# Block attention with a gated feed-forward: probabilities multiplied by their inverse sums ahead of the transpositions, and one gelu handed out earlier

## The chip, the cores and the metric

The kernel runs on one core of a Trainium2 chip. The metric is the device time of the whole program in microseconds (us). A core has five engines with a queue of instructions each: TensorE (PE) for matrix products and transpositions, VectorE (DVE), ScalarE (ACT), GpSimd (POOL) and SyncE (SP), which here only issues the transfers between the chip's memory (HBM) and the core's SBUF. TensorE writes into PSUM, eight banks of 128 partitions by 512 numbers of fp32, and DVE and ACT bring its results from there into SBUF.

## What is computed

Block-causal attention over eight batches of eight heads, 576 positions of 64 numbers, and behind it a gated feed-forward network with a spatial product. Everything is fp32. The reference, cut to what matters (the loads and reshapes are left out):

```python
scores = q @ k.T / sqrt(64)                    # 576 x 576 of each head
scores = where(block_i >= block_j, scores, -1e9)   # blocks of 64 positions
attn = exp(scores - max(scores))
attn = attn / (sum(attn) + 1e-9)
x = attn @ v                                   # (8, 576, 512) over all heads
h = gelu_tanh(x @ w_in)                        # 512 -> 1024
u, v = h[..., :512], h[..., 512:]
v_n = (v - mean(v)) / sqrt(var(v) + 1e-6) * g_ln
v_s = w_sg @ v_n + b_sg                        # over the 576 positions
out = x + (u * v_s) @ w_out
```

The probabilities may be divided by their sums ahead of the product with v, or the product behind it: the result is the same but for rounding.

## The kernel before

**Slots.** The attention goes through 32 slots, n = 0 to 31. A slot is a pair of heads of one batch, so four slots (`Q`) make a batch. Slots 0 to 3 run `opening_slot`, all others `slot`. Products that need fp32 are made of three fp32r products, of a high and a low part of each operand (`kh`, `kl`, `qh`, `ql`, `xh`, `xl`, `gh`, `gl`, `vh`, `vl`), and the low part is a subtraction, mostly on POOL.

**Tiles of probabilities.** The scores of a head lie in five tiles of rows, `prob0` to `prob4`: 64 rows by 64 columns, and then 128 rows by 192, 320, 448 and 576 columns; `pairs[i]` holds both heads' tiles i beside each other. There is one buffer of each, so the scores of slot n + 1 go into the tiles of slot n as soon as those have been transposed. For each tile and head DVE finds the maximum while it moves the scores out of PSUM (`maximum`, which leaves the negative maximum in `negm`), and ACT makes the exponentials in place and their row sums beside them in `sums` (`exponent`).

**A slot, in TensorE's order.** `turn("A0")` and `turn("A1")` transpose the four full blocks of `prob4` of each head into a bank (`pA`), which ACT (A0) and DVE (A1) copy to SBUF (`ptA`). A first hole follows, then `B0` and `B1` (blocks of `prob3` and `prob1`, to `pB` and `ptB`), a second hole, `C` (`prob2`), and `turn_sums`. A third hole, and the scores of slot n + 1: tiles 4, 1 and 0 (`first`). Then the products of slot n with v (`products`, into `ob` and the 64 columns `o0`), `normalise`, and the scores of tiles 3 and 2 (`second`). `inverse` of slot n + 1 and `split_qk(n + 2)` on POOL follow, and a fourth hole. A hole is filled with groups of the feed-forward network of the batch before: 5 groups of v (`accv`), 8 of u (`accu`), 8 of the output of the batch before that (`acco`) and 8 of the spatial product (`accs`). `PLAN` says how many groups each hole of the four slots of a batch takes: "1112", "2114", "2114", "2114".

**The sums.** `inverse` adds 1e-9 to the ten columns of sums, takes the reciprocal (`r`), and ACT spreads each of the ten columns to 64 (`rx`, 128 x 640). `turn_sums` makes ten transpositions: five of the diagonal blocks of `prob` and two of `rx` into the bank `pd`, three of `rx` into the bank `pe`. ACT copies both to `rb` (512 and 384 columns). So `rb` has in each column of positions the inverse sum, along the partitions of the head it belongs to, and `normalise` multiplies `ob` and `o0` by it.

**The side queue.** `side` holds what DVE, ACT and POOL have to do for the feed-forward: an entry "G" for a gelu (of the five tiles `vv`, later of the four tiles `u`), and behind that of v the statistics of its five tiles (`moments`: a `bn_stats` and a `bn_aggr` each), `inverse_std`, the five centrings (`centre`) and the five scalings (`scale`, which makes `vh`, `vl`, `vone` and `vn_t`). `run_gelu` takes a "G" if one stands in front, `run_side(k)` takes up to k other entries and stops at a "G". In `slot`, `run_gelu` is called once, behind the third hole, and `run_side` behind the other three holes with k = 3 (6 in the second batch).

**What sets the order.** TensorE's instructions stay in program order throughout. Those of DVE, ACT and POOL do so in slots 0 to 3; later a scheduler orders them by a timeline of its own, but for the few that are pinned by hand. All calls through a helper (`pin`) carry line 60 in the profile, so tiles, not lines, tell them apart. The banks of PSUM are taken in turn by one name, so a transposition or product waits until the eviction of the tile eight banks earlier is done.

Of the kernel before, what the change touches and what calls it, by code (L numbers as in the profile page):

```python
# [9 lines left out]
F32 = mybir.dt.float32  # L10
# [3 lines left out]
AF = mybir.ActivationFunctionType  # L14
ALU = mybir.AluOpType
# [5 lines left out]
def kernel(  # L21
# [13 lines left out]
    B, H, D, S = qT.shape  # L35
    P = 128
    BLK = 64
# [4 lines left out]
    NT = (S + P - 1) // P  # L42
# [5 lines left out]
    QN = [BLK] + [P] * (NT - 1)  # L48
# [3 lines left out]
    class Engine:  # L52


        def __init__(self, letter, engine):
            self.letter, self.engine = letter, engine
# [5 lines left out]
    vector = Engine("V", nc.vector)  # L62
    scalar = Engine("A", nc.scalar)
    gpsimd = Engine("G", nc.gpsimd)
# [3 lines left out]
    sp = ctx.enter_context(tc.tile_pool(name="sp", bufs=1))  # L68
# [7 lines left out]
    def page(dtype, n, name):  # L76
        tag, bufs = KINDS.get(name, KINDS["w"])
        return sp.tile([P, n], dtype, tag=tag, name=name, bufs=bufs)

    def bank(name):  # L80
        return psum.tile([P, 512], F32, tag="bank", name=name, bufs=8)
# [7 lines left out]
    def turn(out, in_):  # L89
        return tensor.transpose(out, in_, ident)  # L90

    def copy(e, dst, src):
        f = {"v": vector.tensor_copy, "a": scalar.copy, "g": gpsimd.tensor_copy}[e]
        return f(dst, src)
# [9 lines left out]
    def load_qk(n):  # L104
        b, h = PAIRS[n]
        q_f = sp.tile([P, S], F32, tag="q_f", name="q_f", bufs=1)
        k_f = sp.tile([P, S], F32, tag="k_f", name="k_f", bufs=1)
        nc.sync.dma_start(q_f, qT[b, h : h + 2].rearrange("a d s -> (a d) s"))
        nc.sync.dma_start(k_f, kT[b, h : h + 2].rearrange("a d s -> (a d) s"))
        raw[n] = (q_f, k_f)  # L110
# [15 lines left out]
    def load_v(n):  # L126
        b, h = PAIRS[n]
        v_f, v_d = vals[n] = v_bufs[n % 2]
        lo, hi = slice(0, BLK), slice(BLK, P)
        for a, r in ((0, lo), (1, hi)):  # L130
            cols = slice((h + a) * D, (h + a + 1) * D)
            x = v[b, : (NT - 1) * P, cols].rearrange("(j p) d -> p j d", p=P)
            if a == 0:
                nc.sync.dma_start(v_f[:, :, r], x)
            else:
                nc.sync.dma_start(v_f[lo, :, r], x[hi])
                nc.sync.dma_start(v_f[hi, :, r], x[lo])
            nc.sync.dma_start(v_d[r, : NT - 1, r], x[lo])
            nc.sync.dma_start(v_d[r, NT - 1, r], v[b, S - TAIL :, cols])
# [24 lines left out]
    for s in (0, 1):  # L164
        t = cp.tile([P, NT - 1, 2 * D], F32, name=f"v_f{s}")
        d = cp.tile([P, NT, 2 * D], F32, name=f"v_d{s}")
        for a in (0, 1):
            r = slice(a * D, (a + 1) * D)
# [4 lines left out]
    prob = [[pairs[i][:, a * EXT[i] : (a + 1) * EXT[i]] for i in range(NT)] for a in (0, 1)]  # L173
# [120 lines left out]
    def weight_half():  # L294

        while weights:
            said = next(weights[0][1], None)
            if said is not None:
                return said
            weights.popleft()  # L300
# [16 lines left out]
    class Scores:  # L317


        def __init__(self, n):  # L320
            self.qh, self.ql, self.kh, self.kl = qk.pop(n)
            self.sm = sp.tile([P, NT, 2], F32, tag="sums", name="sums", bufs=3)
            gpsimd.memset(self.sm[:, 0, :], 1.0)
            self.negm = [
                sp.tile([P, NT], F32, tag=f"negm{a}", name="negm", bufs=2) for a in (0, 1)
            ]
            self.where = {}
# [44 lines left out]
        def exponent(self, a, i):  # L372
            r, e = slice(0, QN[i]), EXT[i]
            behind["A"] = scalar.activation(
                prob[a][i][r, :e],
                prob[a][i][r, :e],
                AF.Exp,
                bias=self.negm[a][r, i : i + 1],
                scale=-1.0,
                accum_out=self.sm[r, i, a : a + 1],  # L380
            )

        def step(self, *parts):
# [19 lines left out]
        def second(self):  # L403
            self.step((3, 0, EXT[3]))
            self.step((2, 0, EXT[2]))

    TE = {"A0": "a", "A1": "v", "B0": "a", "B1": "v", "C": "v"}
    PLACES = {
        "A0": [(0, 4, j) for j in range(4)],
# [6 lines left out]
    class Values:  # L416
# [9 lines left out]
        def turn(self, which):  # L426
# [3 lines left out]
            for c, (a, i, j) in enumerate(PLACES[which]):  # L430
# [3 lines left out]
                self.pt[a, i, j] = pt[:, c]  # L434
            copy(TE[which], pt, t)

        def inverse(self):

            r = sp.tile([P, NT * 2], F32, tag="ri", name="r", bufs=2)
            vector.tensor_scalar_add(r, self.sm.rearrange("p i a -> p (i a)"), 1e-9)  # L440
            vector.reciprocal(r, r)
            self.rx = sp.tile([P, NT, 2 * D], F32, tag="rx", name="rx", bufs=1)
            scalar.copy(
                self.rx.rearrange("p i (a d) -> p (i a) d", a=2),
                r.unsqueeze(2).broadcast_to([P, NT * 2, D]),
            )

        def turn_sums(self):

            t, t2 = bank("pd"), bank("pe")  # L450
            W = NT * BLK
            for i in range(NT):
                c = slice(i * BLK, i * BLK + P)
                first = turned[:, BLK:] if i else ident
                tensor.transpose(t[:, c], pairs[i][:, P * i : P * (i + 1)], first)
            for i in (0, 1):
                turn(t[:, W + i * BLK : W + i * BLK + P], self.rx[:, i, :])
            for i in (2, 3, 4):
                turn(t2[:, P * (i - 2) : P * (i - 1)], self.rx[:, i, :])
            d = sp.tile([P, W + S], F32, tag="rb", name="rb", bufs=1)  # L460
            copy("a", d[:, :512], t)
            copy("a", d[:, 512:], t2[:, : 3 * P])
            self.dg = [d[:, i * BLK : (i + 1) * BLK] for i in range(NT)]
            self.rb = d[:, W:]
            self.o0 = t2[:, 3 * P : 3 * P + BLK]
# [18 lines left out]
        def normalise(self):  # L484

            x = self.x = page(F32, S, "x")
            vector.tensor_tensor(x[:, BLK:], self.ob, self.rb[:, BLK:], op=ALU.mult)
            vector.tensor_tensor(x[:, :BLK], self.o0, self.rb[:, :BLK], op=ALU.mult)
            spill[self.b, self.p] = dp.tile([P, S], F32, tag="spill", name="spill", bufs=12)
            nc.sync.dma_start(spill[self.b, self.p], x)  # L490

# [14 lines left out]
    def run_side(k):  # L506

        while k > 0 and side and side[0][0] != "G":
            k -= 1
            side.popleft()[1]()  # L510

    def run_gelu():

        if side and side[0][0] == "G":
            side.popleft()[1]()
# [176 lines left out]
    def hole(k=1):  # L692

        while k > 0 and work:
            try:
                next(work[0])
                k -= 1
            except StopIteration:
                work.popleft()
# [17 lines left out]

    PLAN = ["1112", "2114", "2114", "2114"]
    FIRST = ["1112", "1111", "1111", "2114"]
    Q = H // 2  # L720

    def split_pending():

        for f in pending:
            f()
        pending.clear()

    def opening_slot(n, va):
# [17 lines left out]
        weight_half()  # L746
        if n < Q - 1:
            nx.second()
# [11 lines left out]
        nv = Values(n + 1, nx)  # L760
        if n == Q - 1:
            nv.inverse()
# [3 lines left out]
    def slot(n, va):  # L766
        nx = n + 1 < N
        k = 6 if n // Q == 1 else 3
        g = [int(x) for x in (FIRST if n // Q == 1 else PLAN)[n % Q]]
        if n + 1 < N:  # L770
            load_v(n + 1)
        if n + 2 < N:
            load_qk(n + 2)
        va.turn("A0")
        va.turn("A1")
        hole(g[0])
        run_side(k)
        split_pending()
        load_share(n, 0)
        va.turn("B0")  # L780
        va.turn("B1")
        hole(g[1])
        run_side(k)
        va.turn("C")
        va.turn_sums()
        hole(g[2])
        run_gelu()
        load_share(n, 1)
        if nx:
            nx = Scores(n + 1)  # L790
            nx.first()
        va.products()
        va.normalise()
        if nx:
            nx.second()
        load_share(n, 2)
        if n == Q + 1:
            run_side(2 * NT + 1)
        if n % Q == Q - 1:
            va.split()  # L800
        else:
            pending.append(va.split)
        nv = None
        if nx:
            nv = Values(n + 1, nx)
            nv.inverse()
        if n + 2 < N:
            split_qk(n + 2)
        load_share(n, 3)
        for _ in range(g[3]):  # L810
            hole()
            run_side(k)
        return nx, nv
# [68 lines left out]
```

## Time and profile before

| | |
|---|---|
| time, median of 3 runs (lowest to highest) | 758.8 us (758.28 to 758.92) |
| profiled execution | 758.84 us, of it the span 757.0 |
| mean granted TensorE clock | 0.993 of full speed |
| instructions on PE, DVE, ACT, POOL | 6946, 1477, 1064, 376 |
| HBM read, written | 49.98 MB, 18.87 MB |
| transfers' mean rate | 93 GB/s |

The profile is of one execution. A view by groups gives for instructions that are alike their count, their busy time and mean, and the idle time of the engine just before them with what ended it. A view in order of time gives start, duration, engine, line, operation and `out<-in` tiles, with partitions x elements, and in brackets the wait ahead with what ended it. In slots 25 and 26, which begin at 531.8 and 553.9 us, a batch runs its second and third slot; from slot 8 on the four slots of a batch repeat about every 90 us: slots 8, 12, 16, 20, 24 and 28 begin at 147.2, 239.75, 329.79, 419.83, 509.87 and 599.9 us.

### The profile page before, as it was taken

To read this page: it belongs to the slowest core of one execution; us is meant where nothing else is said; L and a number is where in the kernel's file an instruction comes from. 1 tells how busy PE (TensorE), PEld (TensorE's weight loads), DVE (VectorE), ACT (ScalarE), POOL (GpSimd) and SP (SyncE) were. 2 spreads that over 40 slices of the span, in tenths; PEclk is the share of its full clock that TensorE was granted. 3 is DMA by queue.
4 is the path that set the end of the run, shared out by engine and by line. 5 is a ranking of instruction groups with operands and counts; after the bars stand their busy time and mean duration, and the time that the engine had idled before them with its cause. 6 is when DMAs were issued, how large, how long until landed. Compare 5 with 4: busy or idle time off the path is not lost.

```text
span 757.0 us, 18446 instructions
## 1 busy us (share of the span) xinstructions
PE 735.8 (97%) x6946; PEld 693.2 (92%) x6946; DVE 474.8 (63%) x1477; ACT 425.3 (56%) x1064; POOL 305.0 (40%) x376
## 2 busy tenths in 40 slices
PE   8779998999999999999999999999999999999998
PEld 7668998989899899999999899998999989998998
DVE  6988889765855359544785348664495645941732
ACT  5666767457744678337764377544873467721600
POOL 3755697634445323343433334351234532322121
PEclk9979999999999999999999999999999999999999
DMA  6626243333352223322234122521235221120032
GB/s 195 199 69 213 68 121 98 85 95 93 105 160 71 58 79 95 108 69 71 71 118 118 32 71 70 175 75 48 58 85 163 71 57 54 65 78 16 2 126 94
DMA packets 84300, 70.05 MB, mean 93 GB/s; under 512 B 59890, under 2 KB 59890, under 8 KB 84212
## 3 DMA queue, kind: packets, MB, share of 16 engines
q1 hardware_dynamic: 84212, 68.88, 31.0%
q8 instruction: 55, 0.90, 0.5%
q14 instruction: 33, 0.27, 0.1%
HBM read 49.98 MB, written 18.87 MB: 91 GB/s over the span
## 4 chain that ended last, share of the span: by engine, by line
PE 73%; DVE 8%; POOL 5%; DMA 5%; ACT 3%; issue 3%; SPq 2%; DVEq 0%; POOLq 0%; ACTq 0%
PE accs L60 16%; PE acco L60 11%; PE accv L60 11%; PE accu L60 9%; PE s L60 8%; PE ob L60 8%; PE pB L60 3%; PE pA L60 2%; PE pd L60 2%; DVE w L60 2%; ACT prob L60 2%; DVE prob L60 2%; DMA xr<-in_w_out 1%; PE pC L60 1%; POOL rs L60 1%
## 5 line engine op out<-in xcount | busy, mean ns | idle before, releaser
L60 ACT ACTIVATE prob<-prob,negm 128x576 f32<-128x576 f32 (+3 forms) x320 | 176.6, 554 | 70.1 <-DVE negm L60 68.9
L60 DVE CUSTOM_DVE_ANT_0 prob<-s,mask 128x256 f32<-128x256 f32 (+3 forms) x320 | 119.8, 418 | 44.9 <-PE s L60 41.6
L60 POOL TENSOR_TENSOR xh<-x,xh 128x64 fp32r<-128x64 f32 x32 | 10.8, 337 | 196.2 <-DVE xh L60 174.4
L60 POOL TENSOR_TENSOR gl<-u,gh 128x288 fp32r<-128x288 f32 x64 | 52.1, 819 | 88.7 <-DVE gh L60 72.8
L60 PE MATMUL acco<-gh,wo_h 128*128 128x288 f32 x256 | 77.6, 303 | 1.7 <-ACT ptB L60 1.4
L60 PE MATMUL accu<-xh,wi_h 128*128 128x288 f32 x256 | 78.3, 306 | 0.3 <-DVE negm L60 0.3
L60 PE MATMUL accs<-ws_h,vh 128*128 128x288 f32 x256 | 78.0, 305 | 0.0
L60 PE MATMUL accs<-ws_h,vl 128*128 128x288 f32 x256 | 75.5, 295 | 1.7 <-DVE vl L60 1.7
L60 PE MATMUL acco<-gl,wo_h 128*128 128x288 f32 x256 | 75.5, 295 | 0.0
L60 PE MATMUL accu<-xl,wi_h 128*128 128x288 f32 x256 | 75.5, 295 | 0.0
L60 PE MATMUL accs<-ws_l,vh 128*128 128x288 f32 x256 | 75.4, 295 | 0.0
L60 PE MATMUL accu<-xh,wi_l 128*128 128x288 f32 x256 | 75.3, 294 | 0.0
L60 PE MATMUL acco<-gh,wo_l 128*128 128x288 f32 x256 | 75.3, 294 | 0.0
L60 DVE TENSOR_TENSOR u<-accs,u 128x288 f32<-128x288 f32 x64 | 29.2, 457 | 58.3 <-PE accs L60 57.4
L60 PE MATMUL accv<-wi_h,xh 128*128 128x512 f32 x160 | 65.4, 409 | 0.0
L60 PE MATMUL s<-kh,qh 64*128 64x320 f32 (+4 forms) x384 | 64.2, 328 | 0.0
L60 PE MATMUL accv<-wi_l,xh 128*128 128x512 f32 x160 | 62.9, 393 | 0.0
L60 PE MATMUL s<-kh,ql 64*128 64x320 f32 (+4 forms) x384 | 59.8, 305 | 0.9 <-POOL ql L60 0.9
L60 ACT ACTIVATION_READ_ACCUMULATOR prob<-prob,negm 128x1 f32 x320 | 60.0, 188 | 0.0
L60 PE MATMUL s<-kl,qh 64*128 64x320 f32 (+4 forms) x384 | 58.8, 304 | 0.3 <-POOL kl L60 0.3
L60 ACT COPY vv<-accv 128x512 f32<-128x512 f32 x32 | 18.6, 581 | 65.6 <-PE accv L60 65.6
L60 PEld LDWEIGHTS acco<-gh,wo_h 128*128 128x128 f32 x256 | 48.1, 188 | 3.4 <-ACT ptB L60 1.8
(115 smaller groups left out, 2088.5 us busy)
## 6 DMA issues: line engine op xcount, KB each, us to landing
q_f<-in_qT SPq DMA_DIRECT2D x32, 288.0 KB, 3.1
k_f<-in_kT SPq DMA_DIRECT2D x32, 288.0 KB, 3.1
spill<-x SPq DMA_DIRECT2D x32, 288.0 KB, 2.7
xr<-spill SPq DMA_DIRECT2D x32, 288.0 KB, 3.0
out_T<-xr SPq DMA_DIRECT2D x32, 288.0 KB, 2.8
v_f<-in_v SPq DMA_DIRECT2D x32, 128.0 KB, 2.6
v_d<-in_v SPq DMA_DIRECT2D x64, 64.0 KB, 2.7
v_f<-in_v SPq DMA_DIRECT2D x64, 64.0 KB, 2.6
```

Source lines behind the costliest of these rows:

```text
L60: return lambda *a, **k: pin(method(*a, **k), self.letter)
```

## The change

From slot 8 on (`AHEAD = 2 * Q`), the third batch's first slot:

- `inverse` makes the inverse sums in two groups, of tiles 0, 1 and 4 (six columns) and of tiles 2 and 3 (four columns). `SUM` reorders the columns so that each group's lie together; the memset that fills the half-used column of tile 0 moves with it.
- Each tile of each head is multiplied in place by its column of `r`: `prob4` on ACT (two activations with a scale), the four others on DVE (eight `tensor_scalar`).
- `turn_sums` makes only the five diagonal transpositions; ACT copies 320 columns to `rb`; `o0` becomes the last 64 columns of the bank `pd`. The spreading to `rx` and the bank `pe` go.
- `normalise` copies `ob` and `o0` where it multiplied them by `rb`.

In slots 9, 13, 17, 21, 25 and 29, the second of a batch, `run_gelu` is also called behind the first hole: by then v's five groups and two of u's have been issued. So the gelu of v goes into the program there, and `run_side` begins with the statistics in the same slot, where before the "G" was only taken behind that slot's third hole.

```diff
@@ -320,7 +320,7 @@
         def __init__(self, n):
             self.qh, self.ql, self.kh, self.kl = qk.pop(n)
             self.sm = sp.tile([P, NT, 2], F32, tag="sums", name="sums", bufs=3)
-            gpsimd.memset(self.sm[:, 0, :], 1.0)
+            gpsimd.memset(self.sm[:, SUM[0], :], 1.0)
             self.negm = [
                 sp.tile([P, NT], F32, tag=f"negm{a}", name="negm", bufs=2) for a in (0, 1)
             ]
@@ -377,7 +377,7 @@
                 AF.Exp,
                 bias=self.negm[a][r, i : i + 1],
                 scale=-1.0,
-                accum_out=self.sm[r, i, a : a + 1],
+                accum_out=self.sm[r, SUM[i], a : a + 1],
             )
 
         def step(self, *parts):
@@ -404,6 +404,9 @@
             self.step((3, 0, EXT[3]))
             self.step((2, 0, EXT[2]))
 
+    SUM = [0, 1, 3, 4, 2]
+    Q = H // 2
+    AHEAD = 2 * Q
     TE = {"A0": "a", "A1": "v", "B0": "a", "B1": "v", "C": "v"}
     PLACES = {
         "A0": [(0, 4, j) for j in range(4)],
@@ -437,6 +440,21 @@
         def inverse(self):
 
             r = sp.tile([P, NT * 2], F32, tag="ri", name="r", bufs=2)
+            if self.n >= AHEAD:
+                sm = self.sm.rearrange("p i a -> p (i a)")
+                for group in ((0, 1, 4), (2, 3)):
+                    lo, hi = 2 * SUM[group[0]], 2 * SUM[group[-1]] + 2
+                    vector.tensor_scalar_add(r[:, lo:hi], sm[:, lo:hi], 1e-9)
+                    vector.reciprocal(r[:, lo:hi], r[:, lo:hi])
+                    for i in reversed(group):
+                        for a in (0, 1):
+                            x = prob[a][i][: QN[i], :]
+                            y = r[: QN[i], 2 * SUM[i] + a : 2 * SUM[i] + a + 1]
+                            if i == NT - 1:
+                                scalar.activation(x, x, AF.Copy, scale=y)
+                            else:
+                                vector.tensor_scalar(x, x, y, None, op0=ALU.mult)
+                return
             vector.tensor_scalar_add(r, self.sm.rearrange("p i a -> p (i a)"), 1e-9)
             vector.reciprocal(r, r)
             self.rx = sp.tile([P, NT, 2 * D], F32, tag="rx", name="rx", bufs=1)
@@ -447,16 +465,22 @@
 
         def turn_sums(self):
 
-            t, t2 = bank("pd"), bank("pe")
+            t, t2 = bank("pd"), bank("pe") if self.n < AHEAD else None
             W = NT * BLK
             for i in range(NT):
                 c = slice(i * BLK, i * BLK + P)
                 first = turned[:, BLK:] if i else ident
                 tensor.transpose(t[:, c], pairs[i][:, P * i : P * (i + 1)], first)
+            if self.n >= AHEAD:
+                d = sp.tile([P, W + S], F32, tag="rb", name="rb", bufs=1)
+                copy("a", d[:, :W], t[:, :W])
+                self.dg = [d[:, i * BLK : (i + 1) * BLK] for i in range(NT)]
+                self.o0 = t[:, 512 - BLK :]
+                return
             for i in (0, 1):
-                turn(t[:, W + i * BLK : W + i * BLK + P], self.rx[:, i, :])
+                turn(t[:, W + i * BLK : W + i * BLK + P], self.rx[:, SUM[i], :])
             for i in (2, 3, 4):
-                turn(t2[:, P * (i - 2) : P * (i - 1)], self.rx[:, i, :])
+                turn(t2[:, P * (i - 2) : P * (i - 1)], self.rx[:, SUM[i], :])
             d = sp.tile([P, W + S], F32, tag="rb", name="rb", bufs=1)
             copy("a", d[:, :512], t)
             copy("a", d[:, 512:], t2[:, : 3 * P])
@@ -484,8 +508,12 @@
         def normalise(self):
 
             x = self.x = page(F32, S, "x")
-            vector.tensor_tensor(x[:, BLK:], self.ob, self.rb[:, BLK:], op=ALU.mult)
-            vector.tensor_tensor(x[:, :BLK], self.o0, self.rb[:, :BLK], op=ALU.mult)
+            if self.n < AHEAD:
+                vector.tensor_tensor(x[:, BLK:], self.ob, self.rb[:, BLK:], op=ALU.mult)
+                vector.tensor_tensor(x[:, :BLK], self.o0, self.rb[:, :BLK], op=ALU.mult)
+            else:
+                copy("v", x[:, BLK:], self.ob)
+                copy("v", x[:, :BLK], self.o0)
             spill[self.b, self.p] = dp.tile([P, S], F32, tag="spill", name="spill", bufs=12)
             nc.sync.dma_start(spill[self.b, self.p], x)
 
@@ -717,7 +745,6 @@
 
     PLAN = ["1112", "2114", "2114", "2114"]
     FIRST = ["1112", "1111", "1111", "2114"]
-    Q = H // 2
 
     def split_pending():
 
@@ -774,6 +801,8 @@
         va.turn("A0")
         va.turn("A1")
         hole(g[0])
+        if n > 2 * Q and n % Q == 1:
+            run_gelu()
         run_side(k)
         split_pending()
         load_share(n, 0)
```

**DVE at the end of slot 25, before.** The rows stand in the engine's order; `s` is a bank of scores, `x` the output of the slot, `bs` and `stats` the statistics of v, `vl` and `vone` parts of the scaled v, `xr` the residual to which `acco` is added. A number behind `prob_` is that of the buffer: 110 to 114 are tiles 0 to 4. The rows begin behind the last maximum.

```order
L60 TENSOR_SCALAR r<-sums 128x10
L60 RECIPROCAL r<-r 128x10
L567 BN_STATS bs<-vv 128x6
L60 BN_AGGR stats<-bs 128x2
...
L60 COPY ptA_7996<-pA_7995 128x512
L60 BN_AGGR stats<-bs 64x2
L573 SCALAR_TENSOR_TENSOR vv<-vv,stats,g_bc 128x512 x4
L573 SCALAR_TENSOR_TENSOR vv<-vv,stats,g_bc 64x512
```

**DVE at the same place, after.** First the rows between the maxima of the first group and those of the second:

```order
L60 TENSOR_SCALAR r<-sums 128x6
L60 RECIPROCAL r<-r 128x6
L60 TENSOR_SCALAR prob_111<-prob_111,r 128x192
L60 COPY x<-ob 128x512
L60 TENSOR_SCALAR prob_111<-prob_111,r 128x192
L60 TENSOR_SCALAR prob_110<-prob_110,r 64x64
L60 COPY x<-pd 128x64
L60 TENSOR_SCALAR prob_110<-prob_110,r 64x64
L60 ISA prob_113,negm<-s,mask 128x448
```

And those behind the maxima of the second group:

```order
L60 TENSOR_SCALAR r<-sums 128x4
L60 RECIPROCAL r<-r 128x4
L60 TENSOR_SCALAR prob_113<-prob_113,r 128x448 x2
L60 TENSOR_SCALAR prob_112<-prob_112,r 128x320 x2
L601 SCALAR_TENSOR_TENSOR vv<-vv,stats,g_bc 128x512 x4
L601 SCALAR_TENSOR_TENSOR vv<-vv,stats,g_bc 64x512
L60 CAST xh<-x 128x576
L60 SCALAR_TENSOR_TENSOR vl<-vv,rs,vh 128x512 x2
L60 COPY ptA_8076<-pA_8075 128x512
L60 TENSOR_SCALAR vone<-vv,rs 64x512
```

The one small sum of ten columns has become one ahead of the second group's maxima and one behind them, each with its products. The statistics that stood here have moved ahead, into slot 25; the centrings (line 573 before, 601 after) stand directly behind the products, and the first two `vl` now stand ahead of the copy of `pA`.

**ACT from the end of slot 25 into slot 26, before.** `accu` is a group of u, `vh` the high part of the scaled v; the table load stands where the function changes from exponentials and copies to gelu.

```order
L60 COPY u<-accu 128x288
L60 COPY rx<-r 128x640
L60 COPY u<-accu 128x288 x3
L60 ACT_TABLE_LOAD
L60 ACTIVATE u<-u 128x576 x3
L60 COPY ptA_7989<-pA_7988 128x512
L60 ACTIVATE u<-u 128x576
L60 ACTIVATE vh<-vv,rs 128x512
L60 COPY ptB_8052<-pB_8051 128x512
```

**ACT at the same place, after:**

```order
L60 COPY u<-accu 128x288 x3
L60 ACTIVATE vh<-vv,rs 128x512 x2
L60 COPY u<-accu 128x288
L60 ACT_TABLE_LOAD
L60 ACTIVATE u<-u 128x576 x3
L60 COPY ptA_8069<-pA_8068 128x512
L60 ACTIVATE u<-u 128x576
L60 ACTIVATE vh<-vv,rs 128x512
L60 COPY ptB_8120<-pB_8119 128x512
```

Two `vh`, which stood behind the gelus of u and the copy of `pA`, now stand ahead of the table load. POOL's order at this place is the same in both: `kh`, `qh`, `kl`, the memset of the next `sums`, `ql`, and the low parts of `x`.

## The prediction
> **What bounds the kernel now.** I read the page's first part, then the chain of work that ended last, then the chain in order of time.
>
> ```profile
> PE 735.8 (97%) x6946; PEld 693.2 (92%) x6946; DVE 474.8 (63%) x1477; ACT 425.3 (56%) x1064; POOL 305.0 (40%) x376
> ...
> PE 73%; DVE 8%; POOL 5%; DMA 5%; ACT 3%; issue 3%; SPq 2%; DVEq 0%; POOLq 0%; ACTq 0%
> ```
>
> TensorE (PE) is busy for 97% of the span, and the chain stays on it for 73%. The next fence is the chain (start, us, what) in slots 25 and 26, the second and third slot of a batch of four:
>
> ```profile
> 538.51 0.44 PE pC L60 x4
> 538.94 0.77 PE pd L60 x7
> 539.71 0.33 PE pe L60 x3
> 540.04 1.58 PE accu L60 x12
> 541.62 1.58 PE s L60 x22
> 543.20 2.80 PE ob L60 x56
> 545.99 0.12 PE pe L60 x4
> 546.11 1.25 PE s L60 x12
> 547.36 6.55 PE accu L60 x48
> 553.91 0.87 PE pA L60 x8
> 554.78 3.20 PE acco L60 x24
> 557.98 0.87 PE pB L60 x8
> 558.85 1.59 PE acco L60 x12
> 560.44 0.44 PE pC L60 x4
> 560.88 0.76 PE pd L60 x7
> ```
>
> Each piece starts where the one before it ends: TensorE has no gap. So here a TensorE instruction taken away is time saved, until another engine comes too late for the next piece.
>
> **What is removed.** In each of the 24 slots from the ninth on, five transpositions of `rx` go: two of the seven of `pd`, all three of the first `pe` piece. The chain gives 0.77 / 7 = 0.11 us for one of `pd` and 0.33 / 3 = 0.11 for one of `pe`: 0.55 us a slot, 13.2 us in all. A group's mean would mislead:
>
> ```profile
> L60 PE MATMUL pe<-ident,rx 128*128 128x128 f32 x96 | 15.7, 273 | 0.0
> ```
>
> One lasts 273 ns, but they overlap. [...]
>
> Off TensorE, ScalarE (ACT) loses the copy to `rx` and the one from `pe`, and gains two multiplications of 576 columns; these stand between its two groups of exponentials, where it idled (0.97 us below) and will idle longer. The product that normalised becomes a copy of the same 512 columns; I cost it the same (0.69 below). VectorE (DVE) gains one more small sum and reciprocal and eight multiplications a slot.
>
> **What a multiplication costs.** None is in this trace. The nearest row is a product by a number per partition:
>
> ```profile
> 560.80 0.47 DVE L60 TENSOR_SCALAR vone<-vv,rs 64x512 fp32r<-64x512 f32 x1
> ```
>
> 0.47 us for 512 columns and 0.17 for ten (below) give by a straight line 0.43 at 448, 0.36 at 320, 0.28 at 192 and 0.20 at 64; issued back to back they follow about 0.1 us sooner: some 2 us of DVE a slot. The bounds are 0.17 and, from a pass over 448 columns below, 0.62 each. The larger unknown is what they wait for:
>
> ```profile
> 620.37 1.44 POOL L60 TENSOR_TENSOR kl<-k_f,kh 128x576 fp32r<-128x576 f32 x1
> ...
> 620.56 1.27 DVE L60 TENSOR_SCALAR r<-sums 128x10 f32<-128x10 f32 x1 [1.27 <-ACT prob L60]
> ...
> 550.15 0.17 DVE L60 TENSOR_SCALAR r<-sums 128x10 f32<-128x10 f32 x1 [1.21 <-ACT prob L60]
> ```
>
> The same ten-column instruction takes 0.17 us alone, but 1.27 when it starts 0.19 us into GpSimd's (POOL's) `kl`: it ends as `kl` ends. So each multiplication can wait from 0 to 1.45 us. I take the full wait wherever POOL is at work, since the row shows it whole. POOL's work at the end of slot 25 is:
>
> ```profile
> 547.34 0.67 POOL L60 CAST kh<-k_f 128x576 fp32r<-128x576 f32 x1 [13.71 <-PE s L60]
> 547.95 0.67 POOL L60 CAST qh<-q_f 128x576 fp32r<-128x576 f32 x1
> 548.58 1.44 POOL L60 TENSOR_TENSOR kl<-k_f,kh 128x576 fp32r<-128x576 f32 x1
> 550.39 0.10 POOL L60 MEMSET sums<- 128x2 f32 x1 [0.37 <-DVE r L60]
> 550.44 1.45 POOL L60 TENSOR_TENSOR ql<-q_f,qh 128x576 fp32r<-128x576 f32 x1
> ```
>
> Its queue is the same after the change, but the memset now waits for the second small sum, and `ql` starts 0.29 us after that sum (550.44 - 550.15), before the reciprocal is through.
>
> **The walk through slots 25 and 26**, in the profile's clock, with TensorE held at its rows (it runs 1.10 us earlier by the saving, and so does what waits for it):
>
> ```profile
> 546.21 0.69 DVE L60 TENSOR_TENSOR x<-ob,rb 128x512 f32<-128x512 f32 x1 [1.13 <-DMA v_d<-in_v]
> ...
> 546.95 0.62 DVE L60 CUSTOM_DVE_ANT_0 prob<-s,mask 128x448 f32<-128x448 f32 x1
> ...
> 555.52 3.36 DVE L573 SCALAR_TENSOR_TENSOR vv<-vv,stats,g_bc 128x512 f32<-128x512 f32 x5
> ...
> 546.46 0.19 ACT L60 ACTIVATION_READ_ACCUMULATOR prob<-prob,negm 64x1 f32 x1
> ...
> 547.62 0.67 ACT L60 ACTIVATE prob<-prob,negm 128x448 f32<-128x448 f32 x1 [0.97 <-DVE negm L60]
> ...
> 549.93 0.19 ACT L60 ACTIVATION_READ_ACCUMULATOR prob<-prob,negm 128x1 f32 x1
> ...
> 554.36 1.28 ACT L60 ACT_TABLE_LOAD   x1
> 555.66 1.83 ACT L60 ACTIVATE u<-u 128x576 f32<-128x576 f32 x3
> 557.40 0.56 ACT L60 COPY ptA<-pA 128x512 f32<-128x512 f32 x1
> ...
> 558.45 0.71 ACT L60 ACTIVATE vh<-vv,rs 128x512 fp32r<-128x512 f32 x1
> ```
>
> - The first sums are ready at 546.65 (546.46 + 0.19). Small sum and reciprocal take 0.4: the first multiplication runs 547.1 to 547.4. POOL's `kh` follows at once; the copy of `ob` does not wait (0.6). The second multiplication waits for `kh`, the third for `qh`, the fourth for `kl`, which now ends at 550.3.
> - So the maxima of the 448-column tile start at 550.4, not 546.95. ACT's second group of exponentials moves by the same 3.4, from 547.62..550.12 to 551.0..553.5.
> - Second small sum at 553.5. `ql` runs 553.8 to 555.2, the multiplication of the 448 columns waits for it, and the four end at 556.2.
> - Now come the five centrings, 0.67 each (3.36 / 5): first done 556.9, last 559.5. Their statistics no longer stand in front of them: with gelu of v handed out earlier they fill DVE's idle time in slot 25. Without that it would be some 4 us later.
> - On ACT two `vh` now stand ahead of the table load, and the first waits for the first centring: 556.9 + 2 x 0.72, a copy of `u` 0.35, table 1.3, three gelus 1.8, the copy `ptA` 0.5: done at 562.3. `pd` takes over `ptA`'s bank and is due at 560.88. TensorE **waits 1.4 us**.
> - On DVE: `xh` 0.4, two `vl` 1.7 with a wait for POOL, `ptA` 0.6, `vone` 2.2 (it waits for `xl`), two `xr` 0.75, `vl` 0.65, `vn_t` 1.0, `ptB` 0.65: done at 566.3. The scores of slot 26 need that bank at 561.43 (five transpositions of `pd`) + 1.58 + 0.9 = 563.9. That is 2.4 us in all, so **1.0 more**.
>
> The saving of four slots is 2.2 us, so such a batch gains nothing. The other three boundaries between slots have cover: by the same steps the 448-column product ends about 2 us ahead of its transposition in slot 25, where only two groups stand before it, and more elsewhere.
>
> **The sum.** Six batches have this place (slots 8 to 31). Four lose 2.4: 9.6. In the last no memset stands between `kl` and `ql`, so `ql` runs ahead of the second sum and 1.3 of the wait goes: 1.1. In the first, TensorE already waits there now:
>
> ```profile
> L60 PE MATMUL acco<-gh,wo_h 128*128 128x288 f32 x256 | 77.6, 303 | 1.7 <-ACT ptB L60 1.4
> ```
>
> I take 1.5 more there (0.5 to 3, the weights' conversions run beside it). Loss 12.2, saving 13.2, net -1.0. The profiled execution took 758.84 us (span 757.0 and 1.84 around it), 0.04 from the median 758.80. Forecast: **757.8**.
>
> **Rivals.**
> - **The multiplications are covered.** If they do not wait behind POOL as the ten-column sum does, the first centring is 3.2 us earlier (1.9 at the first group, 1.3 at `ql`): both waits vanish and 13.2 us stay: 745.6, up to 749 if some wait is left. For it: the only waits I can show are of other instructions, and the chain of before is gapless there. Against it: the ten-column sum is the same kind of instruction. Chance 0.22.
> - **The queue reaches slot 27 (slower).** In slot 26 three evictions of `acco` stand on DVE behind the multiplications and free the banks of slot 27's B transpositions. By the same walk they are 0.45 us ahead. If one more POOL instruction of 1.45 us gets in per batch than I count, there or in slot 25, each batch pays up to that: 6 x 1.45 = 8.7, 766.5. It decides from 0.45 us on. For it: every figure of the walk is a least one, handovers cost nothing in it. Against it: POOL has no further instruction queued there. Chance 0.18, 765 to 769.
>
> **How the numbers follow.** The forecast has 0.60: its own range, one us either way in a batch's loss, is 752 to 764. A measurement of this kernel tells 0.2% (1.5 us) from no change, so "same" is 757.3 to 760.3. Of the 0.60 I put 0.22 below, 0.20 inside, 0.18 above. Faster is 0.22 + 0.22 = 0.44, same 0.20, slower 0.18 + 0.18 = 0.36. From 747 to 767 about half of the first rival and half of the second stay out, 0.19 together.
>
> **What would show it.** After: `pd` as one piece of 0.55, no first `pe` piece, and slots without a wait 0.55 shorter. Right, if products of `prob` by `r` on DVE last over 1 us where POOL runs `kl` or `ql`, and TensorE's waits name `ptA` and `ptB` once a batch, 1 to 3 us together. Wrong, if these products last under 0.5 throughout, or if TensorE waits at other places, for the products themselves ahead of pB above all.

## The result, and the profile after

The changed kernel took 763.31 us (median of 4, 762.29 to 764.42), the kernel before 758.54 beside it: a ratio of 1.0065, 95% interval 1.0046 to 1.0085. It is slower by 0.65%, where 757.8 was forecast. The profiled execution took 762.61 us, span 760.8.

The page's busy times after, and its shares of the chain that ended last:

```profile
PE 728.7 (96%) x6826; PEld 682.2 (90%) x6826; DVE 591.2 (78%) x1717; ACT 430.1 (57%) x1064; POOL 302.0 (40%) x376
...
PE 63%; DVE 18%; POOL 5%; ACT 4%; DMA 4%; issue 4%; SPq 1%; DVEq 0%; ACTq 0%; POOLq 0%
```

TensorE is busy 7.1 us less, and the chain has gone over from it to VectorE, from 8% to 18%. VectorE works 116 us more. The page has the products among its costliest groups; here is that view for the four shapes apart (count, total us, mean ns, idle before):

```profile
L60 DVE TENSOR_SCALAR prob<-prob,r 128x448 f32<-128x448 f32 x48 | 55.3, 1191 | 0.9
L60 DVE TENSOR_SCALAR prob<-prob,r 128x192 f32<-128x192 f32 x48 | 24.7, 516 | 0.8
L60 DVE TENSOR_SCALAR prob<-prob,r 128x320 f32<-128x320 f32 x48 | 17.8, 410 | 0.0
L60 DVE TENSOR_SCALAR prob<-prob,r 64x64 f32<-64x64 f32 x48 | 17.1, 357 | 0.0
```

What TensorE waits for from slot 12 on, by waits (us in total, times, longest):

```profile
PE pd L60 <- ACT ptA L60: 8.1, 5, 1.7
PE s L60 <- DVE ptB L60: 2.3, 5, 0.5
```

Five batches, five waits of each kind, and nothing else: once a batch, in its third slot. In slot 26:

```profile
555.85 1.03 PE L60 MATMUL pA<-ident,prob 128*128 128x128 f32 x8
...
564.57 0.77 PE L60 MATMUL pd<-ident,prob 128*128 128x128 f32 x5 [1.59 <-ACT ptA L60]
...
568.42 0.41 PE L60 MATMUL s<-kh,qh 64*128 64x320 f32 x1 [0.47 <-DVE ptB L60]
```

The chain in order of time runs from the second small sum to that second wait on VectorE, with the pieces called issue between its instructions:

```profile
554.86 0.74 ACT prob L60 x3
555.60 0.02 issue
555.62 0.18 DVE r L60
555.80 0.02 issue
555.82 0.19 DVE r L60
556.02 0.03 issue
556.04 2.49 DVE prob L60 x4
558.53 3.30 DVE vv L601 x5
...
562.13 1.48 DVE vl L60 x2
...
567.67 0.70 DVE ptB L60
568.37 0.04 issue
568.42 0.96 PE s L60 x8
```

**A ledger.** The executions differ most ahead of slot 8. Slot 4 began between 60.8 and 65.8 us in the profiles of the twelve kernels here, though all issue the same work up to there. So the table counts from the first transposition of slot 8 to TensorE's last end, in the profiled executions, and the times of whole runs stand beside it. It is worked out from TensorE's rows; "a later batch" is slots 20 to 23. Each ratio is to the kernel before as it ran beside that kernel: its median was 758.54 us beside the changed kernel, 758.82 beside e1 to e4, 757.82 beside e5 to e8, and 757.83 beside e9 and e10.

| kernel | median, us | ratio to before (95%) | slots 8 to 11 | a later batch | slot 28 to end | slot 8 to end |
|---|---|---|---|---|---|---|
| before | 758.54 | | 92.53 | 90.04 | 153.74 | 606.43 |
| changed | 763.31 | 1.0065 (1.0046 to 1.0085) | 96.52 | 90.57 | 153.80 | 612.71 |
| e1, gelu alone | 756.80 | 0.9977 (0.9964 to 0.9990) | 91.49 | 90.04 | 153.26 | 604.91 |
| e2, products alone | 776.80 | 1.0235 (1.0214 to 1.0256) | 96.21 | 93.53 | 155.88 | 626.77 |
| e3, products from slot 12 | 760.34 | 1.0026 (1.0012 to 1.0040) | 91.39 | 90.73 | 153.82 | 608.08 |
| e4, four products later | 751.13 | 0.9896 (0.9879 to 0.9912) | 96.51 | 88.19 | 151.09 | 600.35 |
| e5, q and k not split on GpSimd | 751.77 | 0.9907 (0.9883 to 0.9932) | 97.08 | 88.17 | 151.39 | 601.28 |
| e6, eight products left out | 744.92 | 0.9822 (0.9791 to 0.9853) | 91.25 | 87.87 | 151.09 | 593.81 |
| e7, all products on ScalarE | 749.38 | 0.9879 (0.9855 to 0.9903) | 92.00 | 88.40 | 151.63 | 597.24 |
| e8, no w_out | 759.30 | 1.0016 (1.0002 to 1.0031) | 90.72 | 90.57 | 153.80 | 607.20 |
| e9, e3 and e4 together | 746.43 | 0.9850 (0.9827 to 0.9873) | 91.65 | 88.21 | 151.09 | 595.54 |
| e10, e7 from slot 12 | 748.16 | 0.9866 (0.9848 to 0.9883) | 91.48 | 88.40 | 151.62 | 596.75 |

From slot 8 on the change costs 6.28 us: 3.99 in slots 8 to 11, 0.53 to 0.65 in each of the next four batches, 0.06 behind. Ahead of slot 8 this execution was 2.51 us quicker than that of before, 2.47 of it already at slot 4, up to which both issue the same work, so that part is no doing of the change.

### The profile page after: what moved, and what is told of

Read it like the earlier page. It is cut to its first block, busy times and chain, and to the rows that moved or that the text cites. A ratio compares the mean times of both kernels' runs of the same rounds, so it can differ in the third digit from the quotient of the medians.

```text
span 760.8 us, 18339 instructions
## 1 busy us (share of the span) xinstructions
PE 728.7 (96%) x6826; PEld 682.2 (90%) x6826; DVE 591.2 (78%) x1717; ACT 430.1 (57%) x1064; POOL 302.0 (40%) x376
## 4 chain that ended last, share of the span: by engine, by line
PE 63%; DVE 18%; POOL 5%; ACT 4%; DMA 4%; issue 4%; SPq 1%; DVEq 0%; ACTq 0%; POOLq 0%
PE accs L60 15%; PE accv L60 10%; PE acco L60 9%; PE s L60 8%; PE ob L60 8%; PE accu L60 7%; DVE prob L60 6%; ACT prob L60 3%; DVE vv L601 2%; PE pB L60 2%; PE pd L60 2%; PE pA L60 2%; DVE vl L60 2%; DVE w L60 2%; DVE xr L60 1%
## 5 line engine op out<-in xcount | busy, mean ns | idle before, releaser
L60 DVE TENSOR_SCALAR prob<-prob,r 128x192 f32<-128x192 f32 (+1 forms) x192 | 111.0, 619 | 1.7
L60 POOL CAST kh<-k_f 128x576 fp32r<-128x576 f32 x31 | 21.9, 706 | 139.6 <-issue 113.6
L60 PE MATMUL s<-kh,qh 64*128 64x320 f32 (+4 forms) x384 | 66.4, 328 | 2.3 <-DVE ptB L60 2.3
L60 PE MATMUL s<-kh,ql 64*128 64x320 f32 (+4 forms) x384 | 60.8, 306 | 0.7 <-POOL ql L60 0.7
L60 DVE TENSOR_SCALAR r<-sums 128x6 f32<-128x6 f32 (+2 forms) x56 | 20.1, 359 | 51.9 <-ACT prob L60 51.9
L60 POOL TENSOR_TENSOR xh<-x,xh 128x64 fp32r<-128x64 f32 x32 | 13.6, 424 | 103.2 <-DVE xh L60 103.2
```

The source lines that it names most:

```text
L60: return lambda *a, **k: pin(method(*a, **k), self.letter)
```

## The experiments

My theory: the loss comes from the products on VectorE, which wait behind GpSimd's instructions and hold up what follows. The rivals: the earlier gelu with what it reorders on ScalarE; or simply more work on VectorE than there is room for.

**The two halves of the change.** e1 is the kernel before with these two lines ahead of `run_side` behind the first hole, e2 the changed kernel without them:

```diff
+        if n > 2 * Q and n % Q == 1:
+            run_gelu()
```

> The kernel before with the earlier gelu of v alone; no products, all ten transpositions stay. My theory (the loss comes from the products on VectorE, which wait behind GpSimd): VectorE has the statistics out of the way and nothing new, so nothing changes: 757.5 to 759.5 us, no wait of pd or s in slots 26 and 30. Rival (the earlier gelu reorders ScalarE: two vh stand ahead of the table load, the gelus and the copy ptA, and that makes TensorE wait): the wait of pd on ptA shows here too, about 1.6 us a batch, 766 to 770.

> The changed kernel without the earlier gelu of v. My theory: the five statistics (about 3.9 us) stand behind the products again, ahead of the copies ptA and ptB on VectorE; by the trace of the changed kernel ptB is done no sooner than there, the wait of pd goes (ptA on ScalarE stands ahead of vh), the wait of s grows to about 3.2: 763 to 770 us. Rival (the gelu's reordering is the loss, the products are covered): 745 to 752.

e1 has no wait of `pd`, and its later batches take the 90.04 of before: the earlier gelu costs nothing there, though two `vh` stand ahead of the table load in it too. In slots 8 to 11 and at the end it brings 1.5 us together, which I had not expected: 756.8 lies just below my range. So the rival of the gelu falls: alone it costs nothing. Beside the products it does decide where TensorE waits. The products alone cost more than with the gelu, as expected, but 776.8 lies 7 us above my range. From slot 12 on `pd` no longer waits, as I had said. `s` waits 1.14 and 0.19 us in slot 14, where I had said 3.2, and `ob` waits 1.05, which I had not named. The rest is something I had not counted. By stretches (us, busy us of PE and of four other engines, granted clock, DMA share, GB/s), e2 in slot 14:

```profile
292.00:294.00 2.00, 2.00 (x20) 1.84 (x21) 2.00 (x4) 0.00 (x0) 2.00 (x1) 1.00 0.01 4
294.00:296.00 2.00, 0.83 (x9) 0.44 (x7) 2.00 (x4) 0.00 (x0) 1.92 (x2) 1.00 0.00 0
296.00:298.00 2.00, 0.96 (x11) 0.84 (x11) 1.12 (x3) 1.76 (x4) 0.20 (x1) 0.85 0.00 0
298.00:300.00 2.00, 1.83 (x17) 1.84 (x19) 2.00 (x5) 1.79 (x2) 0.00 (x0) 0.50 0.38 147
300.00:302.00 2.00, 2.00 (x26) 2.00 (x25) 2.00 (x11) 1.09 (x4) 0.00 (x0) 0.50 0.33 74
302.00:304.00 2.00, 2.00 (x26) 1.88 (x24) 1.95 (x8) 0.97 (x2) 0.00 (x0) 0.50 0.66 243
304.00:306.00 2.00, 2.00 (x18) 1.77 (x19) 2.00 (x8) 2.00 (x8) 0.79 (x2) 0.94 0.44 110
```

TensorE is busy for 0.83 and 0.96 of two stretches of 2 us; behind them it gets half its clock for some 7 us, and a later batch takes 93.53 us against the changed kernel's 90.57. e2's mean clock is 0.976 against 0.991.

**The third batch.** e3 changes one number, e8 takes the loading and the conversion of w_out away:

```diff
-    AHEAD = 2 * Q
+    AHEAD = 3 * Q
```

```diff
-            ("o", load_weight(w_out, slice(0, DM), wo_h, wo_l, "xr", 0)),
+            ("o", zero_w_out()),
...
-        7: (0, 0, 0, 3),
-        8: (0, 2, 0, 3),
+        7: (0, 1, 0, 0),
```

> The changed kernel with the products only from slot 12 on (AHEAD = 3 * Q): the third batch, slots 8 to 11, keeps the old way. My theory (the third batch alone lost 3.98 us of the profile's difference, since the conversion of w_out runs on GpSimd and VectorE beside it, and each later batch about 0.5): 759.0 to 760.0 us, and the trace's waits of 170, 195 and 198 us are gone. Rival (every batch loses about the same, and the third's loss was the noise of that execution): 762.5 to 763.5.

> The changed kernel without the loading and conversion of w_out: it is set to zero before slot 8, so the network's output is left out of the sum, and the products with zeros take their usual time. My theory (the third batch loses 4 us more than the later ones since GpSimd and VectorE convert w_out there, beside the products of prob): slots 8 to 11 take 90 to 92 us instead of 96.5, as the later batches do, and the waits of pB and of pd at 170 and 198 us shrink to those of the later batches: 757 to 760 us. Rival (it is another plan of the third batch, not the conversion): 96 us and 762 to 764.

Both came out as the theory has it but for the last tenths of e3's median. With w_out at zero the products `acco` did take their usual time: by their three kinds 303, 295 and 294 ns on average, as in the kernel before. Without the products slots 8 to 11 take 91.39, without the loading and conversion 90.72, with both 96.52. Not all of that is their meeting. e6, below, has the conversion and leaves VectorE's eight products out, and its slots 8 to 11 take 91.25, where its later batches take 87.87. Beside that 87.87 the conversion alone costs 3.38, the products alone 2.85 and both 8.65, which is 2.42 more than the two apart. In the changed kernel, at the start of slot 9 (VectorE, GpSimd, TensorE):

```profile
168.65 1.39 DVE L60 TENSOR_SCALAR r<-sums 128x4 f32<-128x4 f32 x1
170.29 3.04 DVE L60 TENSOR_SCALAR prob<-prob,r 128x448 f32<-128x448 f32 x4
...
170.35 1.65 POOL L60 TENSOR_TENSOR ql<-q_f,qh 128x576 fp32r<-128x576 f32 x1
171.97 0.87 POOL L60 TENSOR_TENSOR wo_l<-xr,wo_h 128x256 fp32r<-128x256 f32 x1
...
170.89 0.63 PE L60 MATMUL pB<-ident,prob 128*128 128x128 f32 x4 [0.61 <-DVE prob L60]
172.40 0.63 PE L60 MATMUL pB<-ident,prob 128*128 128x128 f32 x4 [0.89 <-DVE prob L60]
...
201.51 1.03 PE L60 MATMUL pd<-ident,prob 128*128 128x128 f32 x5 [2.96 <-ACT ptA L60]
```

The products are still at it when TensorE wants to transpose them into `pB`, and in slot 10 the wait of `pd` is 2.96 instead of 1.6. Behind that wait TensorE's clock is halved in the changed kernel too (columns as in the stretches of e2):

```profile
200.00:202.00 2.00, 0.49 (x4) 0.49 (x5) 2.00 (x3) 2.00 (x5) 2.00 (x2) 0.97 0.00 0
202.00:204.00 2.00, 2.00 (x10) 2.00 (x9) 1.99 (x5) 1.73 (x4) 0.02 (x1) 0.50 0.00 0
204.00:206.00 2.00, 2.00 (x16) 1.72 (x17) 1.97 (x4) 1.52 (x3) 0.00 (x0) 0.68 0.00 0
```

The twelve products `acco` there take 3.16 us from the first to the next piece, where e6 takes 1.76. e6 has a wait of `pd` in slot 10 as well, and keeps its clock (the products `acco` take 303, 295 and 294 ns on average in it as in the kernel before, and 306, 297 and 297 in the changed kernel):

```profile
197.14 0.76 PE L60 MATMUL pd<-ident,prob 128*128 128x128 f32 x5 [2.38 <-ACT ptA L60]
```

So most of that one wait does not come from VectorE's products. By the starts of the slots, e6 is 3.09 us quicker in slot 9 and 2.22 in slot 10, and within 0.04 the same in slots 8 and 11.

**Order, waiting, or amount of work.** e4 makes the same instructions on the same engines, with the products of tiles 1 and 0 behind the second group's maxima (and the centrings held behind the products, as they stood):

```diff
-                    for i in reversed(group):
+                    for i in (4,) if group[0] == 0 else (1, 0, 3, 2):
...
+                                with tc.issue_after(behind["V"].ins):
+                                    behind["M"] = vector.tensor_scalar(x, x, y, None, op0=ALU.mult)
```

e5 keeps the order and takes GpSimd's q and k away (the centrings held in the same way):

```diff
+            elif n >= AHEAD:
+                copy("a", hi, x)
+                vector.tensor_tensor(lo, x, hi.bitcast(F32), op=ALU.subtract)
```

> The changed kernel with the four products of tiles 1 and 0 held back on VectorE until behind the maxima of the second group; all else keeps its place. Same work, same instructions. My theory (the products wait for GpSimd's kh, qh and kl and hold up the second group's maxima and exponentials, which hold up all that follows): the maxima start 2.4 us sooner, the second group's products end about 2.4 sooner, pd and s wait 0 to 0.5 a batch: 747 to 752 us. Rival (VectorE simply has too much work between slots 25 and 26, wherever it stands): 762 to 764.

> The changed kernel with the splitting of q and k from slot 8 on taken off GpSimd: the high parts are copied on ScalarE, the low parts subtracted on VectorE, which so has 1.4 us more work a slot; products and centrings keep their order. My theory (products last long because they wait for GpSimd's kh, qh, kl and ql): a product of 192 columns takes about 0.3 us, never over 0.6, the four of tiles 3 and 2 take 1.3 us instead of 2.49, all is about 2 us sooner, pd and s wait under 0.7 a batch: 748 to 754 us. Rival (VectorE has too much work): 763 to 768.

Both cures bring a later batch to 88.2 us. In e4 (VectorE; in its execution the same place of slot 25 lies 4.6 us sooner) the maxima of the 448 columns begin 1.05 us behind the first small sum, where the changed kernel needs 3.55:

```profile
544.31 0.17 DVE L60 TENSOR_SCALAR r<-sums 128x6 f32<-128x6 f32 x1 [1.68 <-ACT prob L60]
...
545.36 0.62 DVE L60 CUSTOM_DVE_ANT_0 prob<-s,mask 128x448 f32<-128x448 f32 x1
```

```profile
548.88 0.17 DVE L60 TENSOR_SCALAR r<-sums 128x6 f32<-128x6 f32 x1 [1.67 <-ACT prob L60]
...
550.15 2.06 DVE L60 TENSOR_SCALAR prob<-prob,r 128x192 f32<-128x192 f32 x2
552.13 0.21 DVE L60 COPY x<-pd 128x64 f32<-128x64 f32 x1
552.27 0.23 DVE L60 TENSOR_SCALAR prob<-prob,r 64x64 f32<-64x64 f32 x1
552.43 0.61 DVE L60 CUSTOM_DVE_ANT_0 prob<-s,mask 128x448 f32<-128x448 f32 x1
```

(The second fence is the changed kernel.) With the 2.5 us no `pd` and no `s` waits from slot 12 on. The products do not get shorter by it: VectorE is busy with the four shapes for 116.8 us in e4 and for 114.9 in the changed kernel. They last as long, but where nothing waits for them. In e5 the products have other durations, by groups:

```profile
L60 DVE TENSOR_SCALAR prob<-prob,r 128x448 f32<-128x448 f32 x48 | 23.1, 522 | 0.6
L60 DVE TENSOR_SCALAR prob<-prob,r 128x320 f32<-128x320 f32 x48 | 17.2, 399 | 0.0
L60 DVE TENSOR_SCALAR prob<-prob,r 128x192 f32<-128x192 f32 x48 | 14.5, 314 | 0.6
L60 DVE TENSOR_SCALAR prob<-prob,r 64x64 f32<-64x64 f32 x48 | 11.0, 240 | 0.0
```

0.52 us instead of 1.19 for 448 columns, 0.31 instead of 0.52 for 192: the same instructions, without GpSimd's `kh`, `qh`, `kl` and `ql` beside them. And VectorE has two subtractions a slot more, so the rival of too much work falls. Slots 8 to 11 are not mended by either (96.5 and 97.1): the conversion still runs there. In e5 it costs at another place: slot 8 takes 26.49 us instead of 21.53. There VectorE waits 2.66 us for the transfer of w_out just ahead of the maxima, and TensorE's scores wait 1.87 and 0.58 us for these.

The same is seen from the other side with the products taken off VectorE:

```diff
-                            if i == NT - 1:
+                            if i >= 0:
                                 scalar.activation(x, x, AF.Copy, scale=y)
```

> The changed kernel with all ten products of a slot on ScalarE. My theory: ScalarE's products do not wait for GpSimd (two of 576 columns took 1.45 us beside kh and qh), so the second group's maxima follow at once on VectorE and the centrings need not wait for the products; ScalarE gets about 3.3 us more a slot, and its copy ptA is just in time: 745 to 751 us. Rival (the products' work itself, or their place ahead of the second exponentials, is the loss): pd waits for ptA on ScalarE for 2 us and more a batch: 758 or more.

> The changed kernel without the eight products of VectorE in each slot (tiles 0 to 3 stay without their division, tile 4 keeps it on ScalarE). What the transpositions taken away and the earlier gelu bring when nothing takes their place: 13.2 us and, as the kernel with the earlier gelu alone showed from slot 8 on, 1.5: 743 to 746 us, 87.9 us a batch, no wait of pd or s. If the products' cost were elsewhere (the two groups of sums, the copies of ob), some of the waits would stay: 750 or more.

e7 came out as the theory has it, at 88.40 a batch, with three waits left in slots 8 to 11, of 0.8 (`pB`), 0.9 (`pd`) and 1.2 us (`s`). On ScalarE the two products of 576 columns take 0.77 us each in the changed kernel, e4 and e6 to e8, where GpSimd splits q and k, and 0.77 in e5, where from slot 8 on it does not. VectorE's of 448 columns take 1.19 us on average in the changed kernel and 0.52 in e5. By what means GpSimd holds up the ones and not the others, no run here shows. e6 gives the price of the products: 87.87 a batch is 2.17 below before, the whole saving of four slots. From slot 12 on nothing waits in it, as expected; in slot 10 `pd` still waits 2.38 us and `s` 0.17, which I had not expected. What the transpositions and the gelu could have brought is 12.6 us from slot 8 on, and 744.9 in all.

**The best version.** e9 joins e3 and e4, e10 joins e3 and e7:

> Both cures together: the four products of tiles 1 and 0 held back behind the second group's maxima, and the products only from slot 12 on, so that they do not meet the conversion of w_out. By the two kernels that have one cure each, slots 8 to 11 take 91.4 us instead of 96.5 and the later batches 88.2: five us less than with the first cure alone, 745 to 748 us, no wait of pd over 0.3 us behind slot 12. If the third batch's loss and the later ones were not separate, it would stay near 751.

> All ten products on ScalarE, and only from slot 12 on. The products on ScalarE lost little in the third batch (92.0 us beside 91.4 of the old way there), so 0.6 us sooner than from slot 8 on, and 1 us later than the kernel with both cures: 747 to 750 us.

Both lie in their ranges. e9, at 746.43, is 1.5% below before. By the ratios to before it is 2.1% below the changed kernel. From slot 12 on TensorE waits for nothing there, and it lies 1.7 us (from slot 8) above e6, which leaves the products out.

## Why the prediction was wrong

**What held.** The saving: 0.54 us a slot was forecast as 0.55 (e6: 2.17 in four slots). The price of a wait behind GpSimd: in slot 25 the first product of 448 columns began 0.13 us into `ql` and lasted 1.53 us, where with no `ql` beside it, in e5, one takes 0.52 on average. And the walk through slots 25 and 26. TensorE's rows there lie 2.10 us later than before (`pA` of slot 26 began at 553.75, now at 555.85). Less these 2.10:

| event | forecast | measured |
|---|---|---|
| maxima of the 448 columns begin | 550.4 | 550.33 |
| second small sum | 553.5 | 553.52 |
| products end | 556.2 | 556.43 |
| first centring done (its `vh` begins) | 556.9 | 557.19 |
| `ptA` done on ScalarE | 562.3 | 562.42 |
| `ptB` done on VectorE | 566.3 | 566.26 |

Both waits stand where they were forecast. The last agreement is in part luck. The steps that the prediction lists behind the centrings (559.5) add up to 7.95, so 567.45 and not the 566.3 that it gives. They were too long: by VectorE's starts in slot 26 they took 6.6, above all because `vone` took 1.02 and not 2.2. The two errors cancel. The rival by which the products are covered is refuted for these batches: covered by nothing but another order (e4), another engine (e7) or an idle GpSimd (e5). The rival of slot 27 did not happen: no wait there.

**What failed** is the sum over the batches, in three terms:

- **The first batch**, "I take 1.5 more there (0.5 to 3, the weights' conversions run beside it)". It lost 6.16: 96.52 less the 90.36 that before gives after the saving (92.53 - 2.17). This term, 4.66 us off, turns the sign of the forecast. I had counted one boundary of the batch, the wait that exists there already, and no other. That GpSimd's and VectorE's conversion meets the products ahead of slots 9 and 10 and brings `pB` too late was in no term, though the prediction names it among the signs of being wrong: TensorE waits "for the products themselves ahead of pB". Nor was the half clock behind the wait of 2.96 us, 1.40 us in `acco` alone. e3 and e8 show that most of the loss goes when either the products or the loading and conversion go (91.39 and 90.72). e6 shows that a wait of 2.38 of `pd` in slot 10 is there without VectorE's products; how the rest of the change brings that one about stays open.
- **The last batch**, "so `ql` runs ahead of the second sum and 1.3 of the wait goes". It does run ahead (GpSimd and VectorE in slot 29):

```profile
642.69 1.43 POOL L60 TENSOR_TENSOR ql<-q_f,qh 128x576 fp32r<-128x576 f32 x1
...
642.84 1.33 DVE L60 TENSOR_SCALAR prob<-prob,r 64x64 f32<-64x64 f32 x1
...
647.70 1.41 DVE L60 TENSOR_SCALAR prob<-prob,r 128x448 f32<-128x448 f32 x4
```

  The second group's four take 1.41 instead of 2.49, but one product of 64 columns in the first group now waits for `ql` in their stead, 1.33. The wait moved; 2.23 were lost against 1.1 (153.80 less 153.74 - 2.17).
- **The middle batches**, 2.4 forecast and 2.70 measured (90.57 - 87.87). The profile's idle times, 1.59 and 0.47 in slot 26, give only 2.06 of it, since pieces overlap when none waits (before, `pC` lasts 0.60 from 560.28 and `pd` starts at 560.71), and a late one loses the overlap too. By the starts of TensorE's pieces in slot 26, beside e6, `pd` comes 1.76 later behind `pC`, where 1.4 was taken, and the scores take 0.88 longer, where 1.0 was taken.

4.66 + 1.13 + 1.3 for the four middle batches and 0.2 of the saving are 7.3, from -1.0 to the 6.28 of the ledger. The profile's luck of 2.51 ahead of slot 8 brings that to 3.8 in the profiled execution; the medians say 4.8.

## What to carry to other kernels

In this kernel VectorE's products by a number per partition were priced by what GpSimd ran beside them (0.52 us or 1.19 on average for the same 448 columns), and so was the ten-column sum (0.17 us or 1.27). Price such a one at the worst row, and look at who stands behind it in VectorE's queue. Here the cure was not less work but order: what is needed last goes behind what others wait for. And walk through each kind of batch, not the regular one alone: the term that I guessed, where a one-time conversion ran, was off by 4.66 us, and all that I worked out by 2.6 together.

## What had not been expected of the hardware

In two of the four places below, waits were followed by half of TensorE's clock (0.50 granted). In slot 14 of e2 it was waits of 1.14, 0.19 and 1.05 us within 4 us, 2.38 together, and half the clock for some 7 us. In slot 10 of the changed kernel it was one wait of 2.96, and half the clock for 3.4 us. Others left the clock alone: the waits of 1.59 and 0.47 in slot 26 of the changed kernel (1.00 from 555 to 575 us), and the one wait of 2.38 in slot 10 of e6 (1.00 from 194 to 202 us). So neither the longest wait nor the sum of the waits tells these cases apart. What does, no run here shows.
